# Gated mix of windowed attention and a token MLP: the first Q/K weight rows issued from another queue, no fillers between the transposes of x, another order of the work

## The chip, the core and the metric

The kernel runs on one core of one Trainium2 chip. The metric is device time in microseconds (us), the median of several executions. The core has five engines that run side by side, each with its own list of instructions taken strictly in order: TensorE (PE in the profile; its weight loads are PEld), VectorE (DVE), ScalarE (ACT), GpSimd (POOL), and SyncE (SP), which here only issues DMAs. An engine waits for another through semaphores. TensorE writes to PSUM, which has 8 banks of 128 x 512 fp32; TensorE cannot write a bank again before the engine that empties it is done.

## The reference

x is 2048 tokens by 512, in bf16. Attention and MLP both read it, and a gate per token mixes them.

```python
def _A_ref(x, wqkv, wo):
    B, S, D = x.shape
    H = 32; Dh = D // H; W = 256
    qkv = (lambda x, *d: x.transpose(*d))((x @ wqkv).reshape(B, S, 3, H, Dh), 2, 0, 3, 1, 4)
    q, k, v = qkv[0], qkv[1], qkv[2]
    scores = jnp.einsum("bhqd,bhkd->bhqk", q, k) * (Dh ** -0.5)
    idx = jnp.arange(S)
    mask = (idx[:, None] - idx[None, :] >= 0) & (idx[:, None] - idx[None, :] < W)
    scores = jnp.where(mask[None, None], scores, -1e9)
    p = _softmax(scores, axis=-1)
    o = jnp.einsum("bhqk,bhkd->bhqd", p, v)
    return (lambda x, *d: x.transpose(*d))(o, 0, 2, 1, 3).reshape(B, S, D) @ wo

def _B_ref(x, w1, b1, w2, b2):
    h = _layernorm(x, axis=-1)
    u = jnp.einsum("bsd,sf->bdf", h, w1) + b1
    u = _gelu(u)
    y = jnp.einsum("bdf,fs->bds", u, w2) + b2
    return (lambda x, *d: x.transpose(*d))(y, 0, 2, 1)

g = _sigmoid((x * gate_w).sum(-1, keepdims=True))
return g * a + (1 - g) * b
```

S = 2048, D = 512, F = 1376, 32 heads of 16. The MLP mixes along the tokens: w1 is 2048 x 1376, w2 is 1376 x 2048.

## The kernel before

The tokens are 16 tiles of 128 (`NT`) and 4 blocks of 512 (`NSB`). Everything stays in SBUF once loaded.

**The order is written out by hand.** The kernel first collects tasks (`add`, line 464): each has a name, engines it could run on with a cost, what it depends on, and the buffers it takes. `PLAN` (line 217) lists for every engine the tasks in the order in which that engine is to run them; the engine of a task is the list that it stands in. A number behind a colon is the buffer taken: for TensorE's tasks the PSUM bank (`s0.v0:24` takes the pairs 2-3 and 4-5), for ScalarE's exponentials the SBUF slot. `arrange` (line 104) walks the five lists with estimated costs (`cost_of`, line 91, and the figures in each `add`) and yields one sequence in which the tasks are emitted. The estimates put no instruction into the program. They decide the sequence of emission, and with it, at line 1363, which GpSimd instructions are made to wait for a VectorE instruction that shares its SBUF port.

**The start.** SP loads x in pieces: x0.0 and x0.2 are two tiles each (256 KB), x1.4, x2.8 and x3.12 four tiles each. wqk0 to wqk3 (line 504) are the columns of Q and K of the weight matrix, 128 rows of it each (256 KB), since a projection sums over four chunks of 128 rows; wv is the V part (512 KB), gw the gate's weights. Then come the other three blocks of x, transposed by the DMA (xt1 to xt3), small biases, and w1 in twelve pieces, w2 in eleven, and the copies vs and vz of V rows to other partitions.

TensorE begins with `warm` (line 633), five matmuls of 512 columns on zeros, whose result nobody reads. Block 0 of x is transposed by TensorE: xta0.0.0 and xta0.0.1 need x0.0, xta0.1.0 and xta0.1.1 need x0.2 (in a name the first digit behind the dot is the half of the block's tokens, the second the half of the features); each is four transposes of 128 columns. Between the two halves stands `warmb` (line 656): three matmuls of 256 columns on zeros, placed there by making the second half depend on it. ScalarE or VectorE copies each result out of PSUM (xtc0.0.0 and so on). Then come the four Q and four K projections of block 0, q0_0 to q3_0 and k0_0 to k3_0. Each is a chain of five pieces, `.0` to `.4`: rows of wqk0 with the first and the second half of the tokens (256 columns each), then wqk1, wqk2 and wqk3 with all 512. Their results are copied out by kc (K) and qc (Q; it writes each value twice with a parity mask, 1.21 us).

**The rest.** For every tile j, score tasks `s{j}.v0` to `v3` and `s{j}.C` (the corners of the window) are followed by exponentials on ScalarE (`e`), masks on VectorE or GpSimd (`m`), the products with V (`pv{j}`), and on VectorE a normalisation of five steps (`n1` to `n4` and `nz`). A score task takes two PSUM pairs; each stays taken until its exponential has read it. In between stand the remaining projections, the layernorm's work on VectorE (`bs`, `ba`, `h`), the gate (`gl`), the chains `u0` to `u10` (h times w1, 16 products each), and from the middle on the chains `y` (u times w2, and attention times wo). Each u chain is emptied with its bias by `ub`. All eleven have to be there before `gelu` (line 1296), four instructions on ScalarE which need another table of functions than the exponentials; the y chains then need its result, and each y is finished by `f` and stored by `o`. w2 is loaded over w1's place, so a piece of it can be issued only after the u chains have read what was there.

TensorE runs projections, u and y in one of two forms: whole, or cut into four parts of 32 columns that run side by side (`THEN`, line 315, names after which task). Scores use 32 rows each, four side by side. A task of another form than the one before starts some 0.1 us later.

Of the kernel before, what the change touches and what calls it, by code (L numbers as in the profile page):

```python
# [9 lines left out]
ACT = mybir.ActivationFunctionType  # L10
# [80 lines left out]
def cost_of(t, e):  # L91
    c, n = t.engines[e], t.name
    if e == "PE":
        return c - 0.02 if t.mode == "s" else c * 0.738 if t.mode == "c" else c
# [9 lines left out]
def arrange(tasks):  # L104
# [21 lines left out]
    while len(order) < len(tasks):  # L126
# [92 lines left out]
        warm:5 xta0.0.1:4 xta0.0.0:3 warmb xta0.1.1:4 xta0.1.0:5 q2_0.0:6 q3_0.0:0 k1_0.0:2 k3_0.0:3  # L219
        k0_0.0:1 q1_0.0:5 q1_0.1 k2_0.0:7 q0_0.0:4 k2_0.1 q2_0.1 k0_0.1 q0_0.1 k3_0.1 k0_0.2 q0_0.2 k1_0.1  # L220
        q0_0.3 k3_0.2 q1_0.2 k3_0.3 q1_0.3 q3_0.1 q2_0.2 k1_0.2 q1_0.4 k1_0.3 q0_0.4 k0_0.3 k3_0.4 q2_0.3
        k0_0.4 q3_0.2 q2_0.4 k2_0.2 k1_0.4 k2_0.3 k2_0.4 v1.0:1 q3_0.3 q3_0.4 s0.v0:24 v1.2 v0.0:7 q3_1.0:6
        v0.2 q3_1.2 s0.C:24 v5.0:0 k2_1.0:7 k2_1.2 v5.2 s-1.C:24 v3.0:6 v14.0:7 v14.2 s1.v3:04 biast:3 v3.2
        q1_1.0:7 q1_1.2 s1.v0:02 v2.0:6 v2.2 v12.0:4 v12.2 v4.0:5 v4.2 pv-1.0:0 s0.v1:26 k3_1.0:4 k3_1.2
        k3_2.0:5 s1.v2:06 k3_2.2 v6.0:2 q0_1.0:3 q0_1.2 v6.2 pv0.0:0 pv0.1 pv0.2 s1.v1:46 v7.0:3 v7.2
        v15.0:2 s2.v1:06 v15.2 k0_2.0:5 v13.0:4 k0_2.2 v13.2 k1_1.0:3 s1.C:06 k2_2.0:2 k2_2.2 k1_1.2
        s2.v3:06 k0_1.0:5 k0_1.2 v10.0:2 v10.2 pv1.0:0 pv1.1 pv1.2 pv1.3 s2.v0:46 pv1.4 v8.0:2 v8.2 v9.0:3
        v9.2 s2.v2:06 q2_1.0:5 k1_2.0:4 q2_1.2 s2.C:20 k1_2.2 u0.0:6 u0.2 v11.0:7 v11.2 s3.v1:40 u0.4 u0.6
        u0.8 s3.C:02 u2.0:7 u0.10 u2.2 u0.12 u2.4 s3.v2:42 pv2.0:0 u0.14 pv2.1 pv2.2 pv2.3 u2.6 u2.8
        s3.v0:24 u1.0:6 u1.2 u1.4 s3.v3:02 u1.6 u1.8 u2.10 s4.v0:42 u2.12 u1.10 u2.14 u1.12 u1.14 s4.v1:04  # L230
# [93 lines left out]
def kernel(  # L324
# [171 lines left out]
    def load_t(i):  # L496
# [7 lines left out]
    dqk = [
        load(f"wqk{c}", lambda c=c: nc.sync.dma_start(wqkv[:, c, 0:2 * D], A_wqkv[c * P:(c + 1) * P, 0:2 * D]),
             0.85 if c else 1.65, 2.6)
        for c in range(4)
# [905 lines left out]
```

## Time and profile before

The median of three runs is 199.29 us (199.17 to 199.31). The execution that was profiled took 199.2 us, of which the profile's span covers 197.5.

| what | us |
|---|---|
| profiled execution | 199.2 |
| its span | 197.5 |
| TensorE busy, 14 to 42 / 42 to 119 / 127 to 184.5 | 26.91 of 28 / 74.61 of 77 / 56.27 of 57.5 |
| ScalarE busy in the same stretches | 26.93 / 72.23 / 54.01 |
| VectorE busy in the same stretches | 26.00 / 65.86 / 43.22 |
| x0.0 and x0.2 landed | 3.63 and 4.33 |
| wqk0, wqk1, wqk2, x1.4, wqk3, wv landed | 5.77, 7.02, 7.71, 9.10, 9.72, 12.64 |
| first Q/K matmul, first score matmul (s0.v0) | 5.82, 13.63 |
| xt1 landed | 14.59 |
| last matmul, last output's multiplication | 194.6, 194.63 to 195.04 |

Times of events are counted from the span's start. A busy TensorE is not TensorE at its peak: each matmul is recorded until its result is out, 0.16 us after its successor may start, so back-to-back matmuls of 512 columns last 0.38 us each and start 0.216 apart. The profile records a wait as idle time of an engine ahead of an instruction and names whose semaphore ended it. A DMA has two times, that of its issue on the queue's engine and that of its landing.

The first half microseconds of the DMA traffic, from the table of windows (start and end, length, then each engine's busy time, the granted clock, the DMA engines' share and GB/s):

```profile
2.50:3.00 0.50, 0.50 (x3) 0.00 (x0) 0.00 (x0) 0.00 (x0) 0.45 (x3) 1.00 0.93 330
3.00:3.50 0.50, 0.36 (x1) 0.00 (x0) 0.00 (x0) 0.00 (x0) 0.45 (x3) 1.00 1.09 381
3.50:4.00 0.50, 0.33 (x4) 0.33 (x5) 0.35 (x1) 0.00 (x0) 0.41 (x2) 1.00 1.13 301
4.00:4.50 0.50, 0.50 (x7) 0.50 (x6) 0.47 (x3) 0.18 (x1) 0.48 (x1) 1.00 0.89 152
4.50:5.00 0.50, 0.50 (x6) 0.28 (x5) 0.50 (x2) 0.50 (x2) 0.50 (x1) 1.00 0.73 250
5.00:5.50 0.50, 0.50 (x9) 0.42 (x8) 0.50 (x5) 0.41 (x1) 0.50 (x1) 1.00 1.00 365
```

### The profile page before, as it was taken

Reading aid. Unit: us, or ns where it says so; the run is one execution under the profiler, and the core shown is the slowest. Engines: PE = TensorE matmul, PEld = TensorE weight load, DVE = VectorE, ACT = ScalarE, POOL = GpSimd, SP = SyncE. Lnnn points to the kernel's source line nnn. Section 1 sums busy time; section 2 is a strip of 40 time slices with the busy share of each in tenths; the row PEclk is TensorE's granted clock in tenths of the full one; section 3 lists DMA queues with packets and bytes.
Section 4 is the critical chain, followed back from the end, with each engine's and each line's share of the span. In section 5 each row is a group of like instructions: output and inputs, shape, how many; then the busy total and the mean of one; then the engine's idle time right before and its main releaser. Section 6 shows DMA issues by size and latency. Waiting matters only on the chain.

```text
span 197.5 us, 9026 instructions
## 1 busy us (share of the span) xinstructions
PE 187.4 (95%) x4008; PEld 92.3 (47%) x4040; DVE 157.8 (80%) x340; ACT 169.9 (86%) x200; POOL 64.6 (33%) x102
## 2 busy tenths in 40 slices
PE   7999999999999999999999999899999999999994
PEld 3544344444535344456444563335345354454663
DVE  2699998799999897984767899177955775779893
ACT  3059998999899997999999899998998989899910
POOL 8922796563001122235200420222362320004520
PEclk9999999999999999999999999999999999999999
DMA  5986999942052811001496017001031002003022
GB/s 147 306 212 125 236 328 346 317 123 63 7 156 69 275 62 37 0 3 36 134 391 256 3 39 211 0 5 56 3 109 36 27 9 68 3 3 89 3 98 65
DMA packets 23444, 22.01 MB, mean 111 GB/s; under 512 B 7950, under 2 KB 21518, under 8 KB 23406
## 3 DMA queue, kind: packets, MB, share of 16 engines
q1 hardware_dynamic: 23406, 21.44, 36.1%
q8 instruction: 31, 0.51, 1.1%
q14 instruction: 7, 0.06, 0.1%
HBM read 15.61 MB, written 2.10 MB: 90 GB/s over the span
## 4 chain that ended last, share of the span: by engine, by line
PE 79%; ACT 11%; DVE 4%; issue 3%; DMA 2%; SPq 0%; ACTq 0%
PE pb L708 57%; PE ps L1125 10%; PE ps L980 9%; ACT et L932 7%; PE ps L1080 2%; ACT VA L640 2%; DMA wqkv<-in_A_wqkv_dram 2%; DVE stats L808 1%; ACT L932 1%; DVE et L1216 1%; DVE zt L1233 0%; SPq L489 0%; ACT ug L1291 0%; DVE h L824 0%; PE ps L1036 0%
## 5 line engine op out<-in xcount | busy, mean ns | idle before, releaser
L932 ACT ACTIVATE et<-ps 128x1024 bf16<-128x1024 f32 (+1 forms) x104 | 98.8, 1011 | 8.2 <-PE ps L980 5.5
L571 POOL TENSOR_SCALAR_AFFINE_SELECT et<-et 128x512 bf16<-128x512 bf16 (+3 forms) x60 | 41.6, 704 | 98.4 <-ACT et L932 65.7
L932 ACT ACTIVATE XT<-ps 128x1024 bf16<-128x1024 f32 (+1 forms) x50 | 49.1, 1028 | 1.2 <-PE ps L980 0.7
L708 PEld LDWEIGHTS <-wb 128*32 128x32 bf16 (+4 forms) x663 | 32.5, 97 | 37.0 <-issue 7.0
L708 PE MATMUL pb<-ug,wb 128*32 128x512 bf16 (+6 forms) x344 | 43.9, 365 | 0.9 <-issue 0.6
L708 PE MATMUL pb<-h,wb 128*32 128x512 bf16 (+2 forms) x301 | 41.9, 380 | 1.7 <-issue 1.7
L708 PE MATMUL pb<-XT,wqkv 128*128 128x512 bf16 (+2 forms) x166 | 31.8, 369 | 1.2 <-issue 0.8
L980 PE MATMUL ps<-QZ,KT 32*128 32x256 bf16 (+1 forms) x496 | 23.1, 265 | 0.9 <-ACT et L932 0.8
L1125 PEld LDWEIGHTS <-VA 128*32 128x32 bf16 (+1 forms) x1056 | 20.3, 97 | 6.2 <-issue 1.6
L792 DVE TENSOR_TENSOR QZ<-pb,par 128x1024 bf16<-128x1024 f32 x16 | 19.1, 1213 | 3.3 <-PE pb L708 2.4
L1125 PE MATMUL ps<-et,VA 128*32 128x128 bf16 (+2 forms) x760 | 21.7, 217 | 0.0
L1216 DVE STREAM_TRANSPOSE et<-ps 128x1024 f32<-128x1024 f32 (+1 forms) x13 | 15.7, 1207 | 4.2 <-PE ps L1125 3.7
L1012 DVE TENSOR_TENSOR et<-et,mask 128x512 bf16<-128x512 bf16 x38 | 16.9, 454 | 2.7 <-ACT et L932 2.7
L708 PEld LDWEIGHTS <-wqkv 128*128 128x128 bf16 (+1 forms) x172 | 12.0, 97 | 13.7 <-DMA wqkv<-in_A_wqkv_dram 0.9
L571 POOL TENSOR_SCALAR_AFFINE_SELECT XT<-XT 128x512 bf16<-128x512 bf16 (+1 forms) x15 | 9.8, 659 | 24.5 <-ACT XT L932 13.5
L708 PE MATMUL pb<-wo,xo 128*32 128x512 bf16 (+3 forms) x152 | 17.5, 369 | 0.4 <-issue 0.3
L980 PEld LDWEIGHTS <-KT 32*128 32x128 bf16 x496 | 7.4, 92 | 21.7 <-ACT et L932 12.1
L708 PE MATMUL pb<-wqkv,XT 128*128 128x512 bf16 x60 | 15.8, 380 | 0.6 <-issue 0.3
L1012 DVE TENSOR_TENSOR XT<-XT,mask 128x512 bf16<-128x512 bf16 x20 | 9.7, 485 | 6.4 <-ACT XT L932 6.4
L808 DVE BATCH_NORM_STATS2 stats<-xo 128x6 f32<-128x512 bf16 x16 | 10.6, 675 | 4.2 <-DMA xo<-in_A_x_dram 4.2
L1125 PEld LDWEIGHTS <-VZ 128*32 128x32 bf16 x832 | 13.2, 97 | 0.4
L1125 PE MATMUL ps<-XT,VA 128*32 128x128 bf16 (+2 forms) x296 | 12.7, 217 | 0.1
(77 smaller groups left out, 201.7 us busy)
## 6 DMA issues: line engine op xcount, KB each, us to landing
wb<-in_B_w_dram SPq DMA_DIRECT2D x18, 512.0 KB, 6.6
VZ<-VA SPq DMA_DIRECT2D x26, 70.0 KB, 2.5
xo<-in_A_x_dram SPq DMA_DIRECT2D x3, 512.0 KB, 5.0
wb<-in_B_w_dram SPq DMA_DIRECT2D x4, 352.0 KB, 7.5
out_dram<-ot SPq DMA_DIRECT2D x11, 128.0 KB, 1.8
wqkv<-in_A_wqkv_dram SPq DMA_DIRECT2D x4, 256.0 KB, 5.4
xo<-in_A_x_dram SPq DMA_DIRECT2D x2, 256.0 KB, 2.9
wqkv<-in_A_wqkv_dram SPq DMA_DIRECT2D x1, 512.0 KB, 7.7
```

Source lines behind the costliest of these rows:

```text
L571: return nc.gpsimd.affine_select(out=out_, in_=in_, pattern=[[0, n] for n in pattern] + [[step, HB]], compare_op=op, fill=0.0, base=base_, ...
L640: return nc.scalar.activation(out_(), in_(), ACT.Copy)
L708: made.append(nc.tensor.matmul(buf(b)[c:z_, c0:c0 + w_], lhsT=lhsT[:, c:z_], rhs=rhs, start=(j == 0), stop=(j == n - 1), skip_group_check= ...
L792: lambda k=k, b=b: nc.vector.tensor_tensor(out=QZ[:, k, :, (i % NQ) * SB:(i % NQ + 1) * SB], in0=buf(b)[:, None, :].to_broadcast([P, 2, SB ...
L808: f"bs{t_}", {"DVE": 0.67}, lambda b=b, t_=t_: nc.vector.bn_stats(buf(b)[:], xo[:, t_, :]),
L932: lambda e=e, b=b, shape=shape: nc.scalar.activation(out=shape(buf(e)), in_=shape(buf(b)), func=ACT.Exp, scale=SCALE),
L980: made.append(nc.tensor.matmul(to[:, :, done:done + m], lhsT=keys(j if x == "A" else j - 1, k)[rows], rhs=q[rows], start=True, stop=True, ...
L1012: made.append(nc.vector.tensor_tensor(out=v, in0=v, in1=m.to_broadcast(list(v.shape)), op=ALU.mult))
L1080: made.append(nc.tensor.matmul(buf(b2[r // 2])[m_:m_ + HB, at:at + P], lhsT=keys(t_, k)[rows, a:a + HB], rhs=q[rows], start=True, stop=Tru ...
L1125: return lambda: nc.tensor.matmul(to(), lhsT=v() if callable(v) else v, rhs=buf(e)[rows, col:col + n], start=first, stop=last, tile_positi ...
L1216: lambda: nc.vector.transpose(out=view(buf(tr).bitcast(FP32)), in_=view(buf(o))), [last], takes=[tr], uses=[o],
```

## The change

Four things change in the program.

1. wqk0 is no longer SP's third load but the first instruction in ScalarE's list. On SP the order of the loads becomes x0.0, x0.2, wqk1, wqk2, wqk3, wv, gw, x1.4, xt1, xt3 and then the small biases.
2. `warm` has six matmuls instead of five, and `warmb` is gone: nothing stands between the transposes by dependence.
3. All five lists, and `THEN`, are new. The same tasks are done; some copies, bias rows, masks and final multiplications move between engines (on VectorE 78 masks instead of 85, 6 V copies instead of 5, 6 bias rows instead of 5; on ScalarE 10 V copies instead of 11, 5 bias rows instead of 6, 6 final multiplications instead of 5). xtc0.0.0 goes to VectorE and xtc0.1.0 to ScalarE. w2_9 and w2_10 stand ahead of vz10 on SP.
4. Estimates: `gelu` 7.8 instead of 7.0, a score task 0.01 more, loads of x, wqk1 and w2 a little longer.

The diff, with the lists cut to their beginnings and to the stretch around the GELU:

```diff
-        return c - 0.02 if t.mode == "s" else c * 0.738 if t.mode == "c" else c
+        return c - 0.01 if t.mode == "s" else c * 0.738 if t.mode == "c" else c
...
     PE="""
-        warm:5 xta0.0.1:4 xta0.0.0:3 warmb xta0.1.1:4 xta0.1.0:5 q2_0.0:6 q3_0.0:0 k1_0.0:2 k3_0.0:3
-        k0_0.0:1 q1_0.0:5 q1_0.1 k2_0.0:7 q0_0.0:4 k2_0.1 q2_0.1 k0_0.1 q0_0.1 k3_0.1 k0_0.2 q0_0.2 k1_0.1
+        warm:4 xta0.0.0:3 xta0.0.1:4 xta0.1.0:6 q0_0.0:0 xta0.1.1:3 k3_0.0:2 k0_0.0:1 q3_0.0:5 k1_0.0:6
+        k3_0.1 q3_0.1 q1_0.0:3 q0_0.1 q3_0.2 q3_0.3 q0_0.2 q1_0.1 k0_0.1 q0_0.3 q3_0.4 k3_0.2 q0_0.4 k0_0.2
...
-        q1_3.0:6 u10.12 u10.14 q1_3.2 s10.v0:24 pv7.2 k2_3.0:7 k2_3.2 pv8.0:2 pv8.1 k0_3.0:6 pv8.2 pv8.3
-        pv7.3 k0_3.2 q2_3.0:4 q2_3.2 q3_3.0:5 y4.0:6 y0.0:7 q3_3.2 s9.v1:02 y0.2 y0.4 y4.2 y4.4 y0.6 y4.6
+        u10.14 s10.v0:02 q2_3.0:7 q2_3.2 pv7.3 q3_3.0:2 q3_3.2 pv8.0:0 k0_3.0:3 q1_3.0:6 pv8.1 pv8.2 pv8.3
+        k2_3.0:7 k0_3.2 y0.0:5 q1_3.2 k2_3.2 y0.2 y0.4 y4.0:4 y0.6 y0.8 s9.v1:02 y0.10 y0.11 y0.13 y4.2
...
     ACT="""
-        xtc0.0.1 xtc0.0.0 kc3_0 kc0_0 kc1_0 kc2_0 e0.v0.0:5 e0.v0.1:4 vc0 vc1 e0.C.0:3 e0.C.1:2 kc2_1 vc5
+        wqk0 xtc0.1.0 xtc0.0.1 kc1_0 kc0_0 kc3_0 kc2_0 e0.v0.0:2 e0.v0.1:4 vc1 kc2_1 vc0 e0.C.0:9 e0.C.1:8
...
     DVE="""
-        zeros bs0:0 ba0 bs3:1 const bs1:0 parity ba3 xtc0.1.0 xtc0.1.1 ba1 bs2:1 ba2 bs5:0 bs6:1 ba5 bs7:0
+        zeros parity bs0:1 xtc0.0.0 bs1:0 xtc0.1.1 const ba0 bs2:1 ba2 ba1 bs3:1 ba3 qc0_0 qc3_0 qc1_0 qc2_0
...
     SP="""
-        x0.0 x0.2 wqk0 wqk1 wqk2 x1.4 wqk3 gw wv xt1 bias xt3 vs0 x2.8 vs1 xt2 w1_21 x3.12 w1_00 w1_01 w1_10
+        x0.0 x0.2 wqk1 wqk2 wqk3 wv gw x1.4 xt1 xt3 bias vs1 x2.8 vs0 xt2 w1_03 x3.12 vs2 w1_11 w1_00 w1_12
...
-            d = load(f"x{i}.{t0}", emit, 1.5 if i > 1 else 1.1 if i else 0.75, 2.3 if i else 2.2)
+            d = load(f"x{i}.{t0}", emit, 1.5 if i > 1 else 1.1 if i else 0.8 if t0 else 0.9, 2.3)
...
-    dqk = [
-        load(f"wqk{c}", lambda c=c: nc.sync.dma_start(wqkv[:, c, 0:2 * D], A_wqkv[c * P:(c + 1) * P, 0:2 * D]),
-             0.85 if c else 1.65, 2.6)
-        for c in range(4)
-    ]
+    def load_qk(c, start):
+        return lambda: start(wqkv[:, c, 0:2 * D], A_wqkv[c * P:(c + 1) * P, 0:2 * D])
+
+    dqk = [add("wqk0", {"ACT": 0.5}, load_qk(0, nc.scalar.dma_start), lat=3.2)]
+    dqk += [load(f"wqk{c}", load_qk(c, nc.sync.dma_start), 1.2 if c == 1 else 0.85, 2.6) for c in range(1, 4)]
...
-    add("warm", {"PE": 2.2}, lambda: warming(5, 512), [kz], takes=[wu], ins=10)
+    add("warm", {"PE": 2.62}, lambda: warming(6, 512), [kz], takes=[wu], ins=12)
...
-    between = None
     for n_ in range(2):
-        if n_:
-            between = add("warmb", {"PE": 0.64}, lambda: warming(3, 256), [t], uses=[wu], ins=6)
...
-                [dx[2 * n_], k1, between], takes=[b1], ins=8,
+                [dx[2 * n_], k1], takes=[b1], ins=8,
...
-    gelu = add("gelu", {"ACT": 7.0}, emit_gelu, ub)
+    gelu = add("gelu", {"ACT": 7.8}, emit_gelu, ub)
```

## The prediction

> **What bounds the kernel now.** I read the page's busy times first, then TensorE's own waits from the first Q/K matmul to the last, then its timeline at the start and around the GELU, and ScalarE's and SP's beside them.
>
> ```profile
> PE 187.4 (95%) x4008; PEld 92.3 (47%) x4040; DVE 157.8 (80%) x340; ACT 169.9 (86%) x200; POOL 64.6 (33%) x102
> ...
> PE pb L708 <- issue: 3.8, 24, 0.2
> PE ps L980 <- ACT et L932: 0.8, 3, 0.4
> PE pb L708 <- DMA wqkv<-in_A_wqkv_dram: 0.2, 1, 0.2
> ```
>
> The second to fourth lines are TensorE's waits from 5.8 to 195 us: total, count, longest. The 24 "issue" gaps are mostly holes in the record: 4040 weight loads stand beside 4008 matmuls, and at these gaps a load has no matmul. So from the first Q/K matmul at 5.82 to the last matmul at 194.6 TensorE hardly stops; ScalarE's 0.8 us in three waits is its largest real loss. The time is therefore: when the Q/K chain starts, plus TensorE's own work, plus those few waits, plus 2.9 us from 194.6 to the span's end. ScalarE is close behind (26.93 of the 28 us from 14 to 42 busy, against 26.91 for TensorE), so a cut in TensorE's work alone would be worth little; an earlier start moves both.
>
> ```profile
> 1.04 2.31 PE L626 MATMUL pb<-ug 128*128 128x512 bf16 x5 [1.04 <-DVE ug L553]
> 3.67 1.03 PE L646 MATMUL pb<-ident,xo 128*128 128x128 bf16 x8 [0.31 <-DMA xo<-in_A_x_dram]
> 4.50 0.59 PE L626 MATMUL pb<-ug 128*128 128x256 bf16 x3
> 4.97 0.62 PE L646 MATMUL pb<-ident,xo 128*128 128x128 bf16 x8
> 5.82 3.98 PE L708 MATMUL pb<-XT,wqkv 128*128 128x256 bf16 x25 [0.23 <-DMA wqkv<-in_A_wqkv_dram]
> 9.99 2.75 PE L708 MATMUL pb<-XT,wqkv 128*128 128x512 bf16 x12 [0.19 <-issue]
> ```
>
> TensorE's timeline, start and duration first. Eight transposes take 1.03 us at 3.67 and 0.62 at 4.97: starts 0.107 and 0.056 us apart in the trace, changing at 4.71. Up to there the array runs at half rate, though the profile's row of granted clock reads 1.00 throughout. The chain at 5.82 waits for weights.
>
> ```profile
> 0.79 1.28 ACT L640 ACT_TABLE_LOAD   x1 [0.79 <-PEq L1397]
> ...
> 0.80 0.97 SPq L489 DMA_DIRECT2D xo<-in_A_x_dram  x2
> 1.82 1.41 SPq L505 DMA_DIRECT2D wqkv<-in_A_wqkv_dram  x3
> ...
> 1.82 3.95 DMA wqkv<-in_A_wqkv_dram
> ```
>
> ScalarE's first instruction, SP's first five issues, and the piece of the chain of waits behind 5.82: the first weight rows are issued third on SP and land 3.95 us later, at 5.77.
>
> ```profile
> 114.89 1.28 ACT L1291 ACT_TABLE_LOAD   x1
> 116.18 4.66 ACT L1291 ACTIVATE ug<-ug 128x1536 bf16<-128x1536 bf16 x3
> 120.74 0.61 ACT L1293 ACTIVATE ug<-ug 96x512 bf16<-96x512 bf16 x1
> 121.37 1.28 ACT L932 ACT_TABLE_LOAD   x1
> ...
> 119.83 3.54 PE L708 MATMUL pb<-ug,wb 128*128 128x512 bf16 x15
> 123.75 0.40 PE L980 MATMUL ps<-QZ,KT 32*128 32x256 bf16 x8 [0.38 <-ACT et L932]
> 125.58 0.40 PE L980 MATMUL ps<-QZ,KT 32*128 32x256 bf16 x8 [0.25 <-ACT et L932]
> ```
>
> The GELU holds ScalarE from 114.89 to 122.65, 7.76 us with its two table loads, where the plan counted 7.0. The exponentials behind it come late, and TensorE's next two score visits wait.
>
> **Start.** wqk0 goes to ScalarE, which can issue it at 0.79; with the same 3.95 us it lands at 4.74. The table load slips behind the 0.5 us issue to about 1.3 to 2.6, hidden, since ScalarE's first copy is needed only after 5. On SP each later issue moves up one place, and wv and gw pass x1.4. That is covered: TensorE needed wv only at 12.68, gw's first reader ran at 15.97, and x1.4's readers on VectorE now stand behind the Q copies.
>
> Now x is late. x0.0 landed at 3.63, x0.2 at 4.33, so 256 KB cost 0.70 us; wqk0's 256 KB travel with them, so x0.2 lands between 4.33 and 5.03. I take 4.7, since from 4.0 to 4.5 the engines moved 152 GB/s and in the half microseconds before and after 301 and 250: the weights' slow beginning would now run under x. Four transposes (xta0.1.0) at 0.056 are 0.23, plus 0.25 to start and turn: q0_0.0 at 5.2, bounds 4.9 and 5.8. Its copy of x runs on VectorE behind one bn_stats (0.70) and takes 0.36: done by 5.1.
> - Chain starts at 5.2 instead of 5.82: -0.62.
> - xta0.1.1, four transposes, now lies inside it: +0.23.
> - Waits inside the old chain go: 9.42 to 9.99 instead of 0.22 later for wqk3 (0.36), one bank (0.10), wv (0.10): -0.56.
> - New ones come: q3_0.3 wants wqk2 fourteen instructions in, at some 6.65. wqk2 has SP's fourth place, whose load landed at 7.02: 0.4 late, up to 0.9 with wqk0's traffic. k1_0.0 must also wait until ScalarE has emptied bank 6. I take +0.55.
>
> Sum -0.40. With everything landing early it is -0.62-0.3+0.23-0.56 = -1.25; with no earlier start and new waits only, +0.4.
>
> The Trainium skill (DMA: Bandwidth & Descriptors, "Issuing engines are not separate DMA queues") speaks against this edit: loads from any engine share the same 16 DMA engines, so a second issuer saves only issue time. By it the 768 KB would be complete at 5.03 at the earliest and the term would be about -0.1; the trace's dip at 4.0 to 4.5 is why I don't go that far.
>
> **Fillers.** The first warming grows from five to six matmuls: five start 0.427 apart, so six end near 3.6, before x0.0 is there; nothing. The three fillers (start to start 0.47 in all) leave the path, but x0.2 and not they set its end; nothing more. If the half rate lasted beyond 4.71, this is no longer free: second rival.
>
> **GELU.** The instructions are the same; only the order knows 7.8 us. TensorE's losses there are 0.12 (w2_10 landing at 122.93), 0.46 and 0.32: 0.90, from starts of matmuls against the usual 0.22 and 0.31. In the new order w2_9 and w2_10 stand ahead of vz10 on SP, not behind it, and between s10.v0 and s9.v1 TensorE has five projection chains (0.86 each) and five pieces of y0 (0.43) where it had four and two: some 2.2 us more cover. I take -0.7; bounds -0.9 and +0.4 (another visit left waiting, as the longest now).
>
> **Order.** TensorE's list has the same matmuls. Its changes between full, row-tiled and column-tiled work, each worth about 0.1 (0.31 instead of 0.22 from a projection to a score), number 166 against 165: +0.1. On ScalarE, before the GELU, there is one bias row (0.72) and one V copy (0.62) less; VectorE gets both and loses seven masks (0.45 to 0.49 each) to GpSimd, which at 33% has room for 7 x 0.70. The end is alike: y15m last, its f on VectorE, one DMA. What a new order may add is waits of its own: from -0.16 (the one at 31.75 goes) to +0.8 (as much as all TensorE's waits for ScalarE now); I take +0.2, as an order that planned nothing wrong left 0.16. The changed numbers in the planner's cost and latency tables emit nothing; they reach the program through the order and, at line 1363, through which GpSimd instructions wait for VectorE's port.
>
> Sum: -0.40-0.70+0.10+0.20 = **-0.8 us**. The profiled execution took 199.2 us (span 197.5, 1.7 around it), 0.09 under the median of the runs: 199.2-0.8 = **198.4 us**, its own range 197.5 to 198.9.
>
> **Rivals.**
> 1. The start does not move (0.18). For it: the two queues share DMA engines, and if the table load comes first, wqk0 is issued at 2.07 and lands at 6.02. Against: the engines were not full from 4.0 to 4.5. Then the start's term is about 0 to +0.2: 198.8 to 199.0, say **198.9**.
> 2. Slower, by the clock (0.18). The place is TensorE from 4.7 to 8.4. The fillers kept it issuing between the transposes; without them it stands idle from 3.6 until x0.0 is there and again before x0.2 and the copies. If full rate then comes one period later (3.67 us from the first matmul at 1.04 to 4.71, so 8.4), eight transposes and 3.0 us of the chain run at half rate: 0.4+1.5 = 1.9, less up to 0.55 of waits for weights that this hides. 198.4+1.35 to 1.9 gives 199.7 to 200.3: **200.0**. It decides once half-rate starts last beyond about 6.4. Against: the old start also had 0.52 us without an issue (3.15 to 3.67) and still reached full rate.
> 3. New waits in the order (0.14): an exponential, a copy or a transpose-load due later than planned. For it: ScalarE and VectorE are 96% and 93% busy from 14 to 42, so a visit that is late there is not caught up. Against: their queues carry no more than before. One microsecond lost cancels the gain: **199.2**, 198.7 to 200.
>
> A rule bears on the second rival: the Trainium skill (TensorE: Matmul & The Clock Gate, "What's actually happening") has the array at half rate until a window of about 3.4 us has been busy, and the windows run freely, not from the kernel's start. The 3.67 us here agree. By that rule a late start of the clock would cost up to one more window, an estimated 1.7 us of lost work.
>
> **How the numbers follow.** Forecast 0.50, rivals 0.18, 0.18, 0.14. The range 197.5 to 200.0 holds the forecast's own range, rivals 1 and 3 and the cheaper half of rival 2. A difference of under 0.2%, 0.4 us, can't be told from none for this kernel: below 198.89 lie nearly all of the forecast, half of rival 1 and little else, 0.60; above 199.69 most of rival 2 and a part of 3, 0.19; between, 0.21.
>
> **What would show it.** The first Q/K matmul near 5.2, with wqk0 landed by 4.8; the first score visit (13.63 now) at 13.0 to 13.4; all transposes and Q/K matmuls after 5 at 0.056 and 0.216 apart; the GELU still 7.8 us on ScalarE but no wait of TensorE over 0.2 behind it. The forecast is wrong if the chain begins at 5.8 or later, if 256-column matmuls after 6.4 still start 0.21 apart, or if TensorE's waits for ScalarE between 14 and 185 sum to over 1.5 us.

## The result, and the profile after

The changed kernel takes 201.31 us (median; 201.08 to 201.72) against 199.30 (199.17 to 199.61) for the kernel before beside it: ratio 1.0101, 95% interval 1.0078 to 1.0124. It is slower by 1%, where 198.4 was forecast. On two other occasions the ratio was 1.0073 (1.0043 to 1.0102) and 1.0056 (1.0024 to 1.0089): always slower, by amounts that differ from one occasion to the next; the experiments show part of the reason. The profiled execution took 201.54, its span is 199.8 against 197.5.

TensorE's row on the page of the changed kernel (busy time, share, instructions) is the old one, and only the share has fallen, from 95% to 94%:

```profile
PE 187.4 (94%) x4023; PEld 91.7 (46%) x4055; DVE 156.3 (78%) x334; ACT 169.2 (85%) x199; POOL 74.4 (37%) x111
```

So TensorE does the same work and stands still longer. Its waits from 5 to 194 us (total, count, longest):

```profile
PE pb L704 <- issue: 4.4, 28, 0.2
PE ps L976 <- ACT XT L928: 0.8, 1, 0.8
PE ps L1121 <- DVE VA L640: 0.8, 1, 0.8
PE ps L1121 <- issue: 0.6, 1, 0.6
PE pb L704 <- ACT VA L639: 0.2, 1, 0.2
```

Before there was one line of this size (ScalarE, 0.8 in three waits); now there are three single waits of 0.6 to 0.8. The "issue" line is holes in the record, as the prediction said of its own: a profile of each kernel that has a matmul for every weight load (`before, again` and `changed, third` below) has no such line. Where each of the three stands, and what the stretches between them did, can be read by comparing the start of the same score visit in both traces, at visits ahead of which both orders have done the same work to within 0.12 us:

```
                       before   after   difference  added since the line above
s0.v0 (start)           13.63   13.43     -0.20       -0.20
s2.v2                   42.82   42.99     +0.17       +0.37
s3.v2                   51.53   51.71     +0.18       +0.01
s3.v0                   54.74   55.72     +0.98       +0.80
s8.v1                  105.14  106.09     +0.95       -0.03
s9.C  (GELU between)   127.52  129.09     +1.57       +0.62
s15.B                  185.09  186.73     +1.64       +0.07
last matmul            194.37  196.01     +1.64        0.00
last output's issue    195.07  197.36     +2.29       +0.65
```

The 2.3 us come from four places (14 to 43, 52 to 55, 105 to 127, and the end), and the start gives 0.2 back.

**The start.** TensorE's timeline of the changed kernel (start, duration):

```profile
1.05 2.74 PE L625 MATMUL pb<-ug 128*128 128x512 bf16 x6 [1.05 <-DVE ug L552]
4.42 1.05 PE L645 MATMUL pb<-ident,xo 128*128 128x128 bf16 x12 [0.63 <-DMA xo<-in_A_x_dram]
5.47 0.27 PE L704 MATMUL pb<-XT,wqkv 128*128 128x256 bf16 x1
5.58 0.38 PE L645 MATMUL pb<-ident,xo 128*128 128x128 bf16 x4
5.80 7.26 PE L704 MATMUL pb<-XT,wqkv 128*128 128x256 bf16 x38
```

wqk0, issued at 0.80 from ScalarE, landed at 3.82, ahead of x: x0.0 landed at 4.38 instead of 3.63, x0.2 at 5.03 instead of 4.33. The chain, which needs x transposed and copied, began at 5.47 with one matmul and at 5.80 in earnest. Starts 0.056 apart from 4.5 on show the array at full rate there. Behind 5.80 two waits stand in the chain, 0.22 for weights at 7.16 and 0.04 at 6.16.

**14 to 43.** The chain of waits of the changed kernel between 17 and 26 us (start, duration):

```profile
17.59 5.22 DMA xo<-in_A_x_dram
...
22.91 0.69 DVE stats L804
23.60 0.07 DVE QZ L788
23.67 0.97 issue
24.64 0.24 DVE mv L808 x2
24.88 0.59 DVE VA L640
25.47 0.14 issue
25.60 0.32 PE ps L1121 x32
```

x2.8 lands at 22.82. VectorE's statistics bs10 wait for it, and behind them in VectorE's list stand a Q copy and the V copy vc12 that pv-1.0 needs. TensorE, due at 24.72, goes on at 25.60.

**52 to 55.** TensorE's timeline again:

```profile
53.55 0.23 PE L1121 MATMUL ps<-XT,VZ 128*32 128x64 bf16 x8
53.61 0.23 PE L1121 MATMUL ps<-et,VA 128*32 128x128 bf16 x4
54.46 0.24 PE L1121 MATMUL ps<-XT,VZ 128*32 128x64 bf16 x8 [0.62 <-issue]
```

It stops in the middle of pv2.3, with the same V rows, exponentials and bank in use before and after the stop, and no semaphore ends it.

**The GELU.** ScalarE's timeline, then TensorE's:

```profile
116.83 4.66 ACT L1287 ACTIVATE ug<-ug 128x1536 bf16<-128x1536 bf16 x3
121.40 0.61 ACT L1289 ACTIVATE ug<-ug 96x512 bf16<-96x512 bf16 x1
122.94 1.28 ACT L928 ACT_TABLE_LOAD   x1 [0.92 <-issue]
...
120.20 2.32 PE L704 MATMUL pb<-ug,wb 128*128 128x512 bf16 x10
122.45 0.40 PE L976 MATMUL ps<-QZ,KT 32*128 32x256 bf16 x8
...
125.31 0.40 PE L976 MATMUL ps<-QZ,KT 32*128 32x256 bf16 x8 [0.84 <-ACT XT L928]
```

s9.v3 starts 1.22 after the matmul before it, where 0.31 is usual: 0.91 lost. The GELU ended at 122.01, but the reload of the exponential's table began only at 122.94, when s9.v1, at 122.45, had made its scores (122.85).

What this has to be compared with is less than the 0.90 that the prediction read (0.12, 0.46, 0.32). The last of these is the 0.63 from the start at 124.95 to s9.v2, and one matmul is missing from the record there. The kernel before in its first profile, then in a second one that has all 4040 matmuls:

```profile
124.95 0.38 PE L708 MATMUL pb<-ug,wb 128*128 128x512 bf16 x1
125.58 0.40 PE L980 MATMUL ps<-QZ,KT 32*128 32x256 bf16 x8 [0.25 <-ACT et L932]
...
125.57 0.59 PE L708 MATMUL pb<-ug,wb 128*128 128x512 bf16 x2
126.20 0.40 PE L980 MATMUL ps<-QZ,KT 32*128 32x256 bf16 x8
```

With two matmuls s9.v2 lost 0.10 and not 0.32, and the stretch from s8.v1 to s9.C is equally long in both profiles. So the old order lost 0.68 (0.12, 0.46, 0.10), and the new one 1.01: the first two are gone, 0.91 has come, and s9.v2 still loses 0.10. That is 0.33 of the 0.62 between s8.v1 and s9.C; 0.10 more is lost ahead of s8.v2, and the remaining 0.19 lies in other starts and was not taken apart.

**The end.** VectorE's last instruction and SP's last issues:

```profile
196.33 0.41 DVE L475 TENSOR_SCALAR junk<-pb,c,c 128x128 bf16<-128x128 f32 x1 [2.40 <-PE pb L704]
...
190.50 6.77 SPq L1339 DMA_DIRECT2D out_dram<-ot  x4
197.36 0.38 SPq L1339 DMA_DIRECT2D out_dram<-junk  x1
```

f15m is done at 196.74, but SP issues its DMA at 197.36, 0.62 later; before, it was 0.03. The issue of o15l took 1.28 us instead of 0.34, and o15r and o15m stood behind it. f14, on ScalarE, had waited until 194.14 for its output buffer, whose DMA (o11, issued 190.50) landed at 194.06.

### The profile page after: what moved, and what is told of

Same layout as the page of the kernel before. It is cut to its first block, busy times and chain, and to the rows that moved or that the text cites. A ratio compares the mean times of both kernels' runs of the same rounds, so it can differ in the third digit from the quotient of the medians.

```text
span 199.8 us, 9050 instructions
## 1 busy us (share of the span) xinstructions
PE 187.4 (94%) x4023; PEld 91.7 (46%) x4055; DVE 156.3 (78%) x334; ACT 169.2 (85%) x199; POOL 74.4 (37%) x111
## 4 chain that ended last, share of the span: by engine, by line
PE 85%; DMA 5%; issue 4%; ACT 2%; SPq 1%; DVE 1%; DVEq 0%
PE pb L704 61%; PE ps L1121 11%; PE ps L976 9%; DMA xo<-in_A_x_dram 3%; PE ps L1076 3%; DMA wqkv<-in_A_wqkv_dram 2%; ACT L928 1%; ACT XT L928 1%; ACT et L928 0%; SPq L488 0%; DVE stats L804 0%; PE ps L1032 0%; ACT VA L639 0%; DVE VA L640 0%; SPq L752 0%
## 5 line engine op out<-in xcount | busy, mean ns | idle before, releaser
L928 ACT ACTIVATE et<-ps 128x1024 bf16<-128x1024 f32 (+1 forms) x100 | 95.0, 1017 | 8.0 <-PE ps L976 6.2
L570 POOL TENSOR_SCALAR_AFFINE_SELECT et<-et 128x512 bf16<-128x512 bf16 (+3 forms) x67 | 48.9, 737 | 99.2 <-ACT et L928 50.2
L928 ACT ACTIVATE XT<-ps 128x1024 bf16<-128x1024 f32 (+1 forms) x54 | 52.4, 1016 | 4.5 <-PE ps L976 2.2
L704 PE MATMUL pb<-ug,wb 128*32 128x512 bf16 (+5 forms) x351 | 43.6, 365 | 1.4 <-issue 1.4
L1121 PE MATMUL ps<-et,VA 128*32 128x128 bf16 (+2 forms) x688 | 19.7, 217 | 0.8 <-DVE VA L640 0.8
L1212 DVE STREAM_TRANSPOSE et<-ps 128x1024 f32<-128x1024 f32 x12 | 15.0, 1248 | 4.5 <-PE ps L1121 3.5
L570 POOL TENSOR_SCALAR_AFFINE_SELECT XT<-XT 128x512 bf16<-128x512 bf16 x17 | 12.6, 745 | 12.9 <-DVE et L1008 5.3
L1008 DVE TENSOR_TENSOR XT<-XT,mask 128x512 bf16<-128x512 bf16 x22 | 10.7, 489 | 5.4 <-ACT XT L928 5.3
L1008 DVE TENSOR_TENSOR et<-et,mask 128x512 bf16<-128x512 bf16 x31 | 12.6, 416 | 2.3 <-ACT et L928 2.3
L1121 PE MATMUL ps<-XT,VA 128*32 128x128 bf16 (+2 forms) x368 | 13.4, 216 | 0.0
```

The source lines that it names most:

```text
L570: return nc.gpsimd.affine_select(out=out_, in_=in_, pattern=[[0, n] for n in pattern] + [[step, HB]], compare_op=op, fill=0.0, base=base_, ...
L704: made.append(nc.tensor.matmul(buf(b)[c:z_, c0:c0 + w_], lhsT=lhsT[:, c:z_], rhs=rhs, start=(j == 0), stop=(j == n - 1), skip_group_check= ...
L928: lambda e=e, b=b, shape=shape: nc.scalar.activation(out=shape(buf(e)), in_=shape(buf(b)), func=ACT.Exp, scale=SCALE),
L1008: made.append(nc.vector.tensor_tensor(out=v, in0=v, in1=m.to_broadcast(list(v.shape)), op=ALU.mult))
L1121: return lambda: nc.tensor.matmul(to(), lhsT=v() if callable(v) else v, rhs=buf(e)[rows, col:col + n], start=first, stop=last, tile_positi ...
L1212: lambda: nc.vector.transpose(out=view(buf(tr).bitcast(FP32)), in_=view(buf(o))), [last], takes=[tr], uses=[o],
```

## Experiments

Theory: these are separate places, each with its own cause, and TensorE being gap-free elsewhere, each costs the end what it costs there. Rival: the new order is bound by ScalarE or VectorE, and a wait that is mended comes back as another. The places are read as above, from differences to the first trace before; times scatter by 1 us and more from one execution to the next, so the medians alone could not tell the places apart.

### One visit earlier behind the GELU

```diff
-        y0.2 y0.4 y4.0:4 y0.6 y0.8 s9.v1:02 y0.10
+        y0.2 y0.4 y4.0:4 s9.v1:02 y0.6 y0.8 y0.10
```

> The changed kernel with the score visit s9.v1 moved ahead of y0.6 and y0.8 (0.86 us of TensorE's work), nothing else. Theory 'reload': ScalarE reloads its exponential table only once the first exponential behind the GELU has its scores; in the changed kernel the GELU ended at 122.01, the reload began at 122.94, because s9.v1 ran at 122.45. With s9.v1 at about 121.5 the reload starts at 122.0, s9.v3 follows y at its normal 0.31 instead of 1.22, and the time falls by 0.8 to 0.9, from 201.3 to about 200.45. Rival 'bound elsewhere': the wait is set by the ScalarE work behind the GELU; the wait before s9.v3 shrinks but s9.v2 and s9.C wait instead, as in the kernel before (0.46 and 0.32), and the time falls by 0.2 at most.

Ratio 1.0027 (0.9997 to 1.0058). ScalarE and TensorE in this kernel:

```profile
120.75 0.61 ACT L1289 ACTIVATE ug<-ug 96x512 bf16<-96x512 bf16 x1
121.42 1.28 ACT L928 ACT_TABLE_LOAD   x1
...
120.94 0.40 PE L976 MATMUL ps<-QZ,KT 32*128 32x256 bf16 x8
...
123.80 0.40 PE L976 MATMUL ps<-QZ,KT 32*128 32x256 bf16 x8
```

The reload follows the GELU at once and no visit behind it waits more than the old 0.10. From s8.v1 to s9.C this kernel lost 0.25 less than the one before, where the changed kernel lost 0.62 more: 0.87, as expected. The same 0.62 stands in all eight other profiles of the changed order without this move, and -0.24 to -0.25 in all five with it. This is the steadiest of the losses, and the rival is wrong here. One thing the new order did mend: none of its fourteen profiles has a wait for w2_10, while the old order lost 0.12 and 0.27 to it in its two profiles, and the two below with wqk0 moved show waits of 0.84 and 0.97.

### The stop at 53.84

First TensorE alone is made later, by two pieces of a projection chain:

```diff
-        s3.v2:40 pv2.0:2 pv2.1 u0.14 pv2.2 pv2.3 u2.6 u2.8 s3.v0:04
+        s3.v2:40 u2.6 u2.8 pv2.0:2 pv2.1 u0.14 pv2.2 pv2.3 s3.v0:04
```

> The changed kernel with two projection pieces (u2.6, u2.8: four matmuls, 0.86 us) moved from behind pv2.3 to before pv2.0, so that TensorE comes 0.86 us later to instruction 1489, where it stood still for 0.62 us at 53.84. Theory 'instruction fetch': it stood for its next 16 KB of instructions, asked for some 290 instructions earlier and landed only at 53.22. Then the stop goes: 0.6 to 0.8 less, about 200.6. Rival 'data': it waited for V rows or an exponential of pv2.3; these are done by then, but the stop stays or moves to s3.v0, and the time is within 0.2 of 201.3.

Then TensorE's list stays, and two loads of weights go elsewhere on SP:

```diff
-        vs13 w1_02 w1_23 w1_22 w2_1 wo
+        vs13 w1_02 w2_1 wo
...
-        vz7:0 w2_7
+        vz7:0 w1_23 w1_22 w2_7
```

> The changed kernel with two weight loads (w1_23, w1_22, 352 KB each, issued at 43.85 and 44.40 and landed by 49.65 and 51.10) issued behind vz7, at about 77, instead. TensorE's list is the same. Theory 'fetch behind loads': the fetch at 51.88 to 53.22 was late because weight packets were still ahead of it; before, the same fetch ran at 50.04 to 51.00 with no load in flight. Then the fetch here comes at about 51.0, and the stop of 0.62 at 53.84 goes: 0.6 to 0.8 less, about 200.6. Rival 'dense code': TensorE consumes the 290 instructions of the two pv2 pieces faster than any fetch comes; the stop stays at 0.4 or more.

Ratios 1.0068 (1.004 to 1.0095) and 1.0028 (1.0003 to 1.0053). With the two pieces moved, the stop inside pv2.3 went, but s3.v0 then waited 0.52 for ScalarE's exponentials; from s3.v2 to s3.v0 0.58 was lost instead of 0.80, so this mend mostly exchanged one wait for another. With the loads moved, nothing was lost there at all (0.00), with TensorE's list untouched. The DMA traffic says why. GB/s in 40 slices from 49 to 55 us, in the changed kernel:

```profile
GB/s 94 89 99 99 80 61 42 42 33 23 23 0 0 0 0 0 0 0 0 109 0 0 0 0 0 0 0 0 0 0 0 0 0 0 0 0 0 0 0 0
```

and in the kernel before:

```profile
GB/s 0 0 0 0 0 0 109 0 0 0 0 0 0 0 0 0 0 0 0 0 0 0 0 0 0 0 0 0 0 0 0 0 0 0 109 0 0 0 0 30
```

Each lone slice of 109 is one packet of 16 KB on the queue the page calls "q8 instruction". It has 32 of them, and TensorE's list has 8110 instructions (4055 weight loads and as many matmuls), which fill 32 blocks of 256: they are taken to be TensorE's code. Before, the packet started at 50.04 with no other traffic and was through at 51.00; after, w1_23 and w1_22 were landing until 51.10, the packet started at 51.88 and was through at 53.22, and TensorE, some 230 instructions further on, stood still from 53.84 to 54.46, its weight loads too. In the kernel with the loads moved it started at 49.21, on a timeline that is 0.9 us ahead there:

```profile
GB/s 89 102 82 109 48 41 20 27 0 0 0 0 0 0 0 0 0 0 0 0 0 109 0 0 0 0 0 0 0 0 0 0 0 0 0 0 0 0 0 0
```

(slices from 46 to 52). Over seven profiles with this stretch of the order untouched, 0.80, 1.01, 0.53, 0.80, 0.77, -0.01 and 0.19 were lost from s3.v2 to s3.v0; over five with the loads moved, -0.01 to 0.00. In an eighth untouched one, the kernel with the fillers back (below), nothing was lost there, but 1.21 just ahead, from s2.v2 to s3.v2, most of it in one stop:

```profile
53.01 1.69 PE L707 MATMUL pb<-h,wb 128*128 128x512 bf16 x7 [1.00 <-issue]
```

This supports the reading. The five profiles with a stop over 0.3 in pv2.3 all have 729 weight loads ahead of it, and this one has 601, which is 128 pairs of load and matmul, exactly one block, earlier; and in all six TensorE goes on 1.2 to 1.5 us after the end of a code packet (here 51.49, in the changed kernel 53.22). The stop is thus tied to a place in the code and to its packet, and not to the data of pv2.3. The Trainium skill (Runtime: NRT & Kernel Launch, "Instruction fetch mechanics") has code fetched in blocks of 16 KB, 256 instructions, by a queue of the sequencer's own, and its cost "mostly hidden". The 32 packets agree with the first; the second did not hold here, in a dense stretch of code just after large loads.

### The end

```diff
-        o5 o12 o6 o13 o11 o14
+        o5 o6 o11 o12 o13 o14
```

> The changed kernel with the output DMA of tile 11 issued ahead of those of tiles 12 and 13 on SP; the order of o5, o6 and o12 among them also changes, nothing on another engine. Theory 'output buffer': f14 on ScalarE waits until 194.14 for the landing of o11 (issued 190.50, landed 194.06), which pushes f14, f15l, f15r and their three DMA issues together, and the last issue starts 0.62 after its data is ready. With o11 issued some 9 us earlier f14 starts when y14 is done, near 193.6, and the last issue follows f15m at once: 0.5 to 0.65 less, about 200.7. Rival 'SP's issue': the 1.28 us that SP took to issue o15l is the cause and stays, as f15l and f15r still come from ScalarE behind f14: less than 0.2.

Ratio 1.0053 (1.0024 to 1.0082). From the last matmul to the last issue 0.06 more than before was lost, instead of 0.65. That looks like the expected gain, but it isn't shown to be one: of the eight other profiles with the old order of the outputs, three also lost only 0.05 or 0.06 there, and the others 0.17 to 1.01; and of five with o11 earlier one lost 0.40, because the issue of o15r took 0.95 us although o11 had landed long before f14. What separates good from bad in each is whether one of the last issues on SP takes 0.8 to 1.6 us instead of 0.34. That speaks for the rival, SP's issue: in two of the three good profiles with the old order of the outputs o11 landed 1.75 and 1.80 ahead of the last matmul, even closer to it than in the changed kernel (1.95), and the end lost only 0.06. Why SP's issue takes long, and whether moving o11 makes that rarer, stays open.

### The start, part by part

Four kernels: the changed one with wqk0 back on SP as third load; the changed one with x0.2 on ScalarE's queue in its place and wqk0 second on SP; the kernel before with only wqk0 moved to ScalarE; and the same with seven warming matmuls.

```diff
-    dqk = [add("wqk0", {"ACT": 0.5}, load_qk(0, nc.scalar.dma_start), lat=3.2)]
...
-                nc.sync.dma_start(xo[:, t0:t0 + n_, :], src)
+                (nc.scalar if t0 == 2 else nc.sync).dma_start(xo[:, t0:t0 + n_, :], src)
...
-        x0.0 x0.2 wqk1 wqk2
+        x0.0 wqk0 wqk1 wqk2
```

> The changed kernel with wqk0 put back on SP as third load, all else as changed. Theory 'same bytes': the first three loads (768 KB) share the DMA engines, so the edit only changed who lands first; now x0.0 lands at 3.6, x0.2 at 4.3, wqk0 at 5.8, wqk1 at 7.0. The first Q/K matmul moves from 5.47 to about 5.9, the transposes inside the chain (0.23) are out of the way by then, wqk2 and wqk3 are each a place later: s0.v0 0.2 to 0.6 later than in the changed kernel. Rival 'a microsecond of issue': ScalarE's queue gave the weights a whole microsecond, and s0.v0 comes 0.8 or more later.

> The changed kernel with x0.2 instead of wqk0 on ScalarE's queue, and wqk0 second on SP. Theory 'same bytes': all three have still landed by about 5.0, but now x, which has transposes and copies behind it, is through first (x0.0 and x0.2 by 4.4) and wqk0 last, which the matmuls read as it is. The first Q/K matmul comes at 5.1 to 5.2, with all transposes done: s0.v0 0.3 to 0.5 earlier than in the changed kernel, and so much less time. Rival: a load issued second on SP takes its 3.95 us as before and lands at 5.3; s0.v0 within 0.2 of the changed kernel's 13.43.

> The kernel before with wqk0 on ScalarE's queue and nothing else of the change: its own order, five warming matmuls, fillers between the transposes. Theory 'same bytes': x0.2 lands at 5.0 instead of 4.3, so the last transposes end near 5.6 and the chain starts at 5.8 as before; wqk1 to wqk3 come one place earlier and the 0.36 wait for wqk3 at 9.99 goes: s0.v0 0.2 to 0.4 earlier, time 0.1% to 0.2% less, so the start alone is a small gain and the rest of the change is what costs. Rival 'the forecast': the chain at 5.2, s0.v0 at 13.1, time 0.5 less or better.

> The kernel before with wqk0 on ScalarE's queue, as in the third start run, where full rate came only at 10.3 and s0.v0 2.2 later than before; now with seven warming matmuls instead of five. Theory 'clock': the array stood idle from 3.1 to 4.3 there and the clock's next step came a period later; with the last warming matmul ending at 4.0 full rate comes by 5 and s0.v0 at 13.3 to 13.6 as the loads alone would give, 199.2 in time. Rival 'loads': the weights are what was late; s0.v0 stays 1.5 or more behind.

And the changed kernel with the fillers back, and the kernel before once more:

```diff
+            between = add("warmb", {"PE": 0.64}, lambda: warming(3, 256), [t], uses=[wu], ins=6)
```

> The changed kernel with the three fillers put back between the transposes of x0.0 and of x0.2 (its six warming matmuls stay). The prediction put them at nothing. The start of the changed kernel has had full rate from 4.4 to 6.5 in six profiles, with s0.v0 from 13.16 to 13.74. If the fillers matter for the clock, full rate comes by 5.1 here and s0.v0 at 13.2 to 13.4; if not, or if they stand in the way at half rate (0.64), s0.v0 at 13.4 to 13.9 and the time the same within 0.2%.

> The kernel before, unaltered, for a second look at its start. Theory: with x0.0 landing at 3.6 to 3.7 its array stands idle for only 0.3 us before the first transposes and its fillers keep it busy between them; full rate comes by 5 again (4.71 in the first profile), s0.v0 at 13.5 to 13.8. Rival: full rate comes anywhere from 4.5 to 9 here too, so the clock's chance is no part of the change.

What the profiles show (landings of x0.0, x0.2 and wqk0; the time from which starts are those of full rate; the start of s0.v0; the ratio):

```
                          x0.0  x0.2  wqk0  full rate  s0.v0   ratio
before                    3.63  4.33  5.77     4.7     13.63
before, again             3.54  4.21  7.05     4.4     14.61   1.0008 (0.9983 to 1.0032)
wqk0 back on SP           3.65  4.54  6.45     4.7     14.35   1.0108 (1.0069 to 1.0146)
changed                   4.38  5.03  3.82     4.5     13.43   1.0101 (1.0078 to 1.0124)
x0.2 on ScalarE's queue   4.12  4.46  5.13     5.9     13.37   1.0021 (0.9994 to 1.0048)
before, wqk0 on ScalarE   4.25  5.06  3.75    10.3     15.83   1.0040 (1.0019 to 1.0061)
the same, seven warming   4.47  5.15  3.96     6.4     14.35   0.9999 (0.9980 to 1.0019)
changed, fillers back     4.69  5.34  4.18     8.8     15.35   1.0119 (1.0080 to 1.0159)
```

Two things are in this table. First, the three loads are through by 5.0 to 5.3 whenever two queues issue them, and 5.8 to 7.1 when SP issues all three; the load issued last lands last. With wqk0 on ScalarE x is late, with x0.2 there the weights are: in neither does the chain start at 5.2 with everything at hand at full rate. The rule that loads from any engine share the same DMA engines (the Trainium skill, DMA: Bandwidth & Descriptors, "Issuing engines are not separate DMA queues") led the prediction to put the 768 KB at 5.03 at the earliest, and x0.2 did land at 5.03 in the changed kernel. The second queue had all three through 0.4 to 2.0 earlier than SP alone. Issue time is 1.02 of that (wqk0 issued at 0.80 instead of 1.82); with the scatter of wqk0 on SP, 5.77 to 7.05, it is not shown whether the second queue saves more.

So much for the theory; its numbers fared badly. With wqk0 back on SP s0.v0 came 0.92 later than in the changed kernel's profile and 0.71 later than its mean over eight profiles (13.64), not 0.2 to 0.6, because wqk0 landed at 6.45 and not at 5.8: the first figure is the rival's (0.8 or more), the second lies between the two. With x0.2 on ScalarE's queue the loads landed as expected, but s0.v0 came only 0.06 earlier: the array was at half rate until 5.9.

Second, the clock. The kernel before with wqk0 on ScalarE, expected to gain 0.2 to 0.4, lost 2.2 by s0.v0. Its TensorE timeline:

```profile
4.30 1.03 PE L646 MATMUL pb<-ident,xo 128*128 128x128 bf16 x8 [0.94 <-DMA xo<-in_A_x_dram]
5.12 0.85 PE L626 MATMUL pb<-ug 128*128 128x256 bf16 x3
5.76 1.06 PE L646 MATMUL pb<-ident,xo 128*128 128x128 bf16 x8
6.62 8.41 PE L708 MATMUL pb<-XT,wqkv 128*128 128x256 bf16 x37
```

The second eight transposes take 1.06 as the first do, not 0.62 as before, and the chain's 37 matmuls 8.41: half rate up to 10.3. In the eight profiles with the changed start as it stands, full rate came at 4.4, 4.4, 4.5, 4.8, 5.1, 6.0, 6.5 and 9.4, and s0.v0 between 13.16 and 15.20. Where x0.0 lands by 3.7 (the kernel before twice, and wqk0 back on SP) it came at 4.4 to 4.7 each time. The fillers do not secure it (8.8 with them), nor does a seventh matmul (4.6, 6.4 and 6.6). In the old order two more warming matmuls did take the ratio from 1.0040 to 0.9999, two intervals that just meet, so they may make a late step rarer. What secures full rate was not found, and that a late x is what delays it is not shown: only three profiles have an early x.

### The mends together

Three of the moves above (s9.v1, the w1 loads, o11), and on VectorE

```diff
-        qc3_1 ba7 vc14 bs5:1 biasc ba6 bs10:0 qc1_1 ba5 ba10 vc12 bs11:0
+        qc3_1 ba7 vc14 bs5:1 biasc ba6 qc1_1 ba5 vc12 bs10:0 ba10 bs11:0
```

first with the changed start, then with x0.2 on ScalarE's queue and seven warming matmuls, then with each of these two alone; and the changed kernel unaltered, twice.

> The changed kernel with four moves in its order and nothing else: s9.v1 ahead of y0.6, o11 ahead of o12 and o13 on SP, w1_23 and w1_22 behind vz7 (as in the three runs above), and on VectorE bs10 and ba10 behind vc12, so that a late x2.8 does not hold up the V copy that TensorE waits for at 24.4. Theory 'separate places': the gains add: 0.86 behind the GELU, 0.6 to 0.8 at the fetch, 0.4 to 0.6 at the end, 0 to 0.4 at 24.4, together 1.9 to 2.4 under the changed kernel and 0.2 to 0.6 under the kernel before; no wait of TensorE over 0.3 between 14 and 194 us. Rival 'bound elsewhere': a quarter or more of it comes back as other waits, and the time stays above the kernel before.

> The four mends, with x0.2 instead of wqk0 on ScalarE's queue and seven warming matmuls instead of six. The x0.2 run had x landed by 4.46 and wqk0 by 5.13, but its array ran at half rate until 5.9; with the seventh matmul the array is idle for 0.3 instead of 0.6 to 1.2 us before the first transposes. If the idle time is what put the clock off, full rate comes by 4.9 and s0.v0 at 12.9 to 13.1, 0.4 less than with the four mends alone. If the clock's time is chance, s0.v0 is at 13.1 to 13.7.

> The four mends with seven warming matmuls instead of six, wqk0 on ScalarE's queue as changed. The four mends alone had ratio 0.9974, with full rate only at 9.37 in the profiled execution. Theory 'clock': the idle time of the array ahead of the first transposes (0.7 us there) is what lets full rate slip; with 0.3 us idle it comes by 5 every time, s0.v0 at 13.2 to 13.5, ratio 0.9955 to 0.9965. Rival 'chance': full rate still comes anywhere from 4.4 to 9.4, and the ratio stays at 0.997 to 0.998.

> The four mends with x0.2 instead of wqk0 on ScalarE's queue and the six warming matmuls of the change. Theory 'clock': what m2_four_mends_x02 gained over the four mends came from the seventh matmul, so this one has ratio 0.9970 to 0.9980, with full rate at 5 to 6.5. Theory 'order of loads': x through first is worth 0.2 to 0.4 by itself, ratio 0.9955 to 0.9965.

> The changed kernel itself, unaltered, beside the three below on the same chip. If the traces' places hold, its times lie 1.5 to 2.3 above the kernel before; that part of its losses which depends on when a load lands (x2.8 before 24.4 us, o11 before f14, the fetch at 52) makes its times spread wider than those of the kernel before.

> The changed kernel once more, for its start and its four places: full rate between 4.4 and 9.4, s0.v0 13.2 to 15.2, the wait of 0.9 behind the GELU and the stop of 0.6 to 0.8 at the fetch as in every profile so far.

```
                              us     ratio to before
four mends                  198.97   0.9974 (0.9959 to 0.9988)
and x0.2, seven warming     198.63   0.9957 (0.9941 to 0.9974)
and seven warming           198.78   0.9956 (0.9935 to 0.9976)
and x0.2                    198.84   0.9966 (0.9948 to 0.9985)
changed, again              200.99   1.0073 (1.0043 to 1.0102)
changed, third              200.36   1.0056 (1.0024 to 1.0089)
```

The changed kernel itself lies 1.24 and 0.77 above the kernel before in these two, less than the 1.5 to 2.3 expected; its places scatter as said (the fetch cost 0.80 and 0.19 there, the end 0.78 and 0.69; the third run has no stop over 0.3 at the fetch), and only the 0.62 around the GELU is the same every time.

The mends add up. TensorE's waits from 5 to 194 us with the four mends are

```profile
PE pb L704 <- issue: 4.3, 27, 0.2
PE pb L704 <- ACT VA L639: 0.3, 2, 0.2
```

and nothing that was mended came back. The VectorE move is seen where x2.8 is late: it landed at 24.52 in this profile and at 24.50 in the one with the fillers back, on timelines equally late; there pv-1.0 waited 0.64, here not at all. Without the move the wait was 0.88 and 0.97 when x2.8 landed at 22.8 and 22.9, 0.25 at 22.5, and nothing at 21.5 and 21.7. Where that wait is absent, the new order gains 0.5 from s0.v0 to s2.v2, in all four mended kernels alike.

The four mended kernels are all faster than the one before. Among themselves they can't be told apart, and full rate came at 9.4, 4.6, 6.6 and 6.8 in their profiles, so neither the theory that the idle array sets the clock's time nor the one on the order of the loads is shown. The four mends' profiled execution is its slowest (200.14), with 1.57 lost by s0.v0.

## Why the prediction was wrong

**What bounds the kernel** was right: TensorE's work is the same, the time is the start, the waits and the end, and a wait that was mended stayed mended up to the last matmul.

**Start, -0.40.** Measured -0.20 at s0.v0, inside the bounds -1.25 to +0.4, but three of the four terms were off. The chain started at 5.47 and not at 5.2: wqk0 landed at 3.82, even earlier than the 4.74 assumed, and took its time from x, which came at 5.03, the upper bound and not the 4.7 chosen. That is -0.35 instead of -0.62. The transposes inside it cost 0.22 (0.23 forecast). The old chain's waits were -0.34 and not -0.56: between 9.42 and 9.99 the record misses a matmul (21 of 512 columns ahead of the V chain, 22 in the second profile of this kernel), so 0.14 was lost there and not 0.36. The new waits were 0.26 and not 0.55. Together -0.21. Over the eight profiles of this start s0.v0 has a mean of 13.64, against 13.63 and 14.61 before: about the rule's -0.1 or rival 1's zero, set against a kernel before whose weights scatter. That the move pays is not shown: alone in the kernel before it gave a ratio of 1.0040 (1.0019 to 1.0061).

**Fillers, 0.** Not shown either way: with them back the ratio is 1.0119, without them 1.0056 to 1.0101, and the clock's chance is larger than the difference.

**GELU, -0.70.** This step failed most: +0.33 was measured, 1.03 off. Only 0.68 was there to gain, since the 0.32 held a matmul missing from the record and was 0.10. The 2.2 us more cover were there, and 0.12 and 0.46 went. But the cover was put ahead of s9.v1, and s9.v1 was not only work that waits for ScalarE: ScalarE's table reload waited for it, and 0.91 was lost at s9.v3. The bound of +0.4, "another visit left waiting", named the kind and held; the row that would have priced it (the reload at 121.37, straight behind the GELU, because the scores already lay there) was shown and not asked what it depends on.

**Order, +0.10.** Of the 0.62 from s8.v1 to s9.C, 0.29 is left beside the GELU's waits: 0.10 ahead of s8.v2 and 0.19 in other starts. Against that the new order gains 0.5 from 14 to 43 when no load is late. The count of changes, 166 against 165, was a poor measure of either.

**New waits, +0.20, bound +0.8.** Measured +0.37 to s2.v2 (a late x2.8) and +0.80 at the fetch, 1.17 together, 0.97 off. Neither was in the working: the waits behind VectorE's list were taken to be no more than before without following what each statistic waits for, and TensorE's own code was no resource in the sum, though the page has a row for it.

**"The end is alike", 0.** Measured +0.65. The last y chain, its f on VectorE and one DMA were alike, as written; but SP's issues ahead of that DMA were not in the working, and one of them took 1.28 instead of 0.34. Six of nine profiles with the changed order of the outputs show a loss there; the cause of the long issue stays open.

Sum of the stretches: -0.20+0.37+0.01+0.80-0.03+0.62+0.07+0.65 = 2.29. By the forecast's terms it is start -0.20, GELU +0.33, order +0.29, new waits +1.17, the end +0.65 and 0.05 besides, against -0.8.

**Rivals.** The third, new waits in the order, is what happened, with its price of one microsecond less than half of the truth, as the end and the GELU came on top. The second, the clock, fell in the profiled execution (4.5, not 8.4). A late step does occur with this start: half rate lasted up to 6.0, 6.5 and 9.4 in three of eight profiles.

## What to carry to other kernels

Before a load is moved to a second queue, ask which of the loads in flight has work behind it before it is useful, and issue that one early: the load issued last landed last here, and wqk0, moved ahead, made x 0.7 us later. When an order is searched anew around a longer instruction, look at what the next instruction on that engine waits for: work moved ahead of it as cover can keep away what it waits for. Before a gap is priced, count the matmuls around it: a hole in the record looks like a wait of 0.22. And in a kernel bound by one engine with thousands of unrolled instructions, that engine's code is a load like the others: here it helped to keep large transfers out of the microseconds ahead of a dense stretch.

## What was not expected of the hardware

- TensorE ran out of code for 0.62 us in the profiled execution: a block of 256 instructions landed 2.2 us later than in the kernel before, after loads of 352 KB that landed up to 51.10.
- Full rate came at 4.4 to 10.3 us with the array's first matmul always at 1.04 to 1.06, and the pages' rows of granted clock show nothing of it (0.9 or more in every slice of the start). The Trainium skill (TensorE: Matmul & The Clock Gate, "What's actually happening") lets the point vary by about half a microsecond with the phase of a free-running window; here it varied by almost six.
- ScalarE's table reload did not run ahead: it started when the input of the activation behind it was there. It stood 0.92 us idle in between.
- One DMA issue on SP takes 0.33 to 0.6 us as a rule and now and then 0.8 to 1.9 (o15l 1.28, x2.8 1.86); in the changed kernel's profile the same 128 KB of output lands 1.9 to 3.8 us after its issue.
